# Scratch stores of a fused attention and two-MLP kernel: issued by GpSimd's queue instead of SyncE's

## The chip, the core and the metric

The kernel runs on one core of a Trainium2 chip. The core has TensorE (PE in the profile), VectorE (DVE), ScalarE (ACT), GpSimd (POOL) and SyncE (SP), each with its own in-order queue of instructions, and 16 DMA engines that they share. The metric is the time of one execution in device microseconds. Three runs of the kernel before gave 866.27, 866.44 and 866.68 us; the median is 866.44.

## The reference

Three stages, all in float32. `q`, `k`, `v` are drawn for 4 batches, 8 heads, 576 positions and a head size of 64.

```
scores = (q @ k^T) / 8, only where 0 <= row - column < 64, else -1e9
attn   = softmax(scores) @ v               -> x: 2304 tokens x 512
h = x @ w_in   (512 x 2048);  r = max(h, 0);  x = (r * r) @ w_out   (2048 x 512)
h = x @ w2_in  (512 x 2048);  g = max(h, 0) + log1p(exp(-|h|));  out = g @ w2_out
```

## The kernel before

**Precision.** Every matmul operand of the two MLPs is held as two float32r parts, a high part and the rest ("split"), and each product takes three matmuls: high x high, high x low, low x high. For a weight this split is made on ScalarE and VectorE in `add_weights`: `magnitude` (ACT, L498), `hold` and `shift` (DVE, L501 and L505, one input each), `top` and `bottom` (DVE, L511 and L517, two inputs), `hi` (ACT, L524) and `lo` (DVE, L528). There are 32 weight pieces per MLP: 16 of `w_in` (index 0 in the names) and 16 of `w_out` (index 1).

**Stages.** The attention works on 18 pairs of 64-row windows. The first MLP takes the tokens in five tiles of 384, 384, 512, 512 and 512. For the first two tiles the split weights of the first MLP stay in SBUF and are used there directly (matmuls L841, L842, L844 into `h`, then L863 into `acc`). While this goes on, each split weight is also stored to scratch memory in HBM: `w_in` to `d_in` (tiles `di...`) and `w_out` to `d_out` (tiles `do...`). Then sums and differences of quarters of `w_in` are made (`add_sums`, L570 to L601) and stored there as well: from the third tile on, the first product is done by a scheme with seven instead of eight products of half-size blocks, which needs these sums. From then on the weights come back from `di` and `do` through two rings of SBUF buffers (`ri`, loaded at L1277, and `ro`, loaded at L1285). The results of the first MLP go to scratch `yd` (L970) and are loaded for the second MLP at L987. The weights of the second MLP are split the same way, but later, in the middle of the first MLP's work, through three slots of an SBUF `area`: a slot is loaded (L474 or L479), split in place, stored, and free for the next weight only when that store has landed.

**What sets the order.** A planner (`Plan`) orders all work before the program is emitted, from written-down costs, due times (`WANTED`) and shifts (`SHIFT`). Every engine then runs its instructions in that order, and an instruction that waits holds up all behind it on its engine. In the kernel before, all DMAs are issued by SyncE (`nc.sync.dma_start`): loads and stores stand in one queue. A DMA also waits until the eighth DMA before it on its queue kind has landed, since eight semaphores serve each kind in turn.

**The stores.** There are 176 store instructions to scratch: `put_mats` (L467, two a call) for the pieces of `w_in` with an even number and for the sums; L536 for those with an odd number; L533 for `w_out`; and L970 for the first MLP's results (8 for the two tiles of 384, 24 for the three of 512, which are cut at the edges of the second MLP's tiles). GpSimd only builds an identity matrix and masks at the start.

Of the kernel before, what the change touches and what calls it, by code (L numbers as in the profile page):

```python
# [148 lines left out]
class Plan:  # L149
# [16 lines left out]
    def add(self, key, on, fn, after=(), rank=None, take=(), give=(), lag=0.17, close=(), choice=None, opens=(), then=None):  # L166
        j = Job()
        j.key, j.fn, j.rank, j.lag = key, fn, rank, lag
        j.on = dict(on)
        j.choice = choice  # L170
        j.close = list(close)
        j.opens = list(opens)
        j.after = [a for a in after if a is not None]
        j.take, j.give = list(take), list(give)
        j.then, j.nexts = then, []
        j.got, j.users, j.start, j.end, j.ready, j.who = {}, [], None, None, 0.0, None
        assert key not in self.jobs, key
        self.jobs[key] = j
        return key
# [117 lines left out]
def window_attention_moe_moe2(  # L297
# [22 lines left out]
    nc = tc.nc  # L320
# [10 lines left out]
    Q = 2 * P  # L331
# [18 lines left out]
    def f32(ap):  # L350
        return ap.bitcast(F32)
# [54 lines left out]
    live = {}  # L406
    whole = {"area": area}

    def place(j, name, shape, dtype):

        s = j.got[name]
        if isinstance(s, tuple):
            n = 1
            for d in shape[1:]:
                n *= d
            t = whole[s[0]][:, s[1]:s[1] + n]
            if dtype is not F32:
                t = t.bitcast(dtype)
            if len(shape) == 3:
                t = t.rearrange("p (a b) -> p a b", a=shape[1])  # L420
        else:
            of = ppool if s[0] == "p" else wpool if s[0] == "w" else pool
            t = of.tile(shape, dtype, tag=s, name=name.replace(".", "_"))
        live[name] = t
        return t
# [7 lines left out]
    def copy(e, out, in_):  # L433
        (nc.scalar.copy if e == "ACT" else nc.vector.tensor_copy)(out=out, in_=in_)  # L434
# [4 lines left out]
    def as_float(word):  # L439
# [11 lines left out]
    MAT = (  # L451
        {"A": 0, "T2": 1, "T3": 2, "T1": 3, "B": 4, "C": 5, "T4": 6},
        {"A": 0, "T1": 1, "B": 2, "T2": 3, "T3": 4, "T4": 5, "C": 6},
    )
    d_in = {
        (ph, b): dpool.tile([P, 7, 2, Q], F32, tag=f"di{ph}_{b}", name=f"di{ph}_{b}") for ph in range(2) for b in range(NB)
    }
    d_out = {
        (ph, b): dpool.tile([P, 2, 2, DM], F32, tag=f"do{ph}_{b}", name=f"do{ph}_{b}") for ph in range(2) for b in range(NB)
    }  # L460
# [3 lines left out]
    def put_mats(b, ph, first, step, t):  # L464

        for i in range(2):
            nc.sync.dma_start(  # L467
                out=d_in[ph, b][:, first:first + step + 1:step, i], in_=f32(t[:, i]).rearrange("p (m f) -> p m f", m=2)
            )

    def load_raw(t, ph, f, which):
        src = (W_IN, W_OUT)[which][ph].bitcast(U32)
        if which == 0:
            nc.sync.dma_start(  # L474
                out=t.rearrange("p (c f) w -> p c (f w)", c=KC),
                in_=src[:, f * 2 * P:(f + 1) * 2 * P].rearrange("(c p) f -> p c f", p=P),
            )
        else:
            nc.sync.dma_start(out=t.rearrange("p f w -> p (f w)"), in_=src[f * P:(f + 1) * P, :])  # L479

    def add_weights(ph, n, f, which, want):

        me = f"{ph}_{f}_{which}"
        z = f"z{me}"
        raw = f"raw{me}"

        def load(j):
            if ph:
                t = place(j, raw, [P, 2 * DM], F32)
                live["w" + me] = t.bitcast(F32R).rearrange("p (s f) -> p s f", s=2)  # L490
                t = t.bitcast(U32).rearrange("p (f w) -> p f w", w=2)
            else:
                t = wpool.tile([P, DM, 2], U32, tag=f"w{which}_{f}", name=raw)
            live[raw] = t
            load_raw(t, ph, f, which)

        def magnitude(j):
            nc.scalar.activation(out=place(j, z, [P, DM], F32), in_=live[raw][:, :, 1].bitcast(F32), func=AF.Abs)  # L498

        def hold(j):  # L500
            nc.vector.tensor_scalar(out=live[z], in0=live[z], scalar1=HUGE, scalar2=TINY, op0=ALU.min, op1=ALU.max)  # L501

        def shift(j):
            u = live[z].bitcast(U32)
            nc.vector.tensor_scalar(  # L505
                out=u, in0=u, scalar1=3, scalar2=0x3FFFFFFF, op0=ALU.logical_shift_left, op1=ALU.bitwise_and
            )

        def top(j):
            u = live[z].bitcast(U32)  # L510
            nc.vector.scalar_tensor_tensor(  # L511
                out=u, in0=live[raw][:, :, 1], scalar=0xC0000000, in1=u, op0=ALU.bitwise_and, op1=ALU.bitwise_or
            )

        def bottom(j):
            u = live[z].bitcast(U32)
            nc.vector.scalar_tensor_tensor(  # L517
                out=u, in0=live[raw][:, :, 0], scalar=29, in1=u, op0=ALU.logical_shift_right, op1=ALU.bitwise_or
            )

        def hi(j):
            if not ph:
                wt[f, which] = live["w" + me] = wpool.tile([P, 2, DM], F32R, tag=f"w{which}_{f}", name=f"w{me}")
            nc.scalar.copy(out=live["w" + me][:, 0], in_=live[z])  # L524

        def lo(j):
            t = live["w" + me]
            nc.vector.tensor_tensor(out=t[:, 1], in0=live[z], in1=f32(t[:, 0]), op=ALU.subtract)  # L528

        def store(j):  # L530
            t = live["w" + me]
            if which:
                nc.sync.dma_start(out=d_out[ph, f // 2][:, f % 2], in_=f32(t))  # L533
            elif f % 2:

                nc.sync.dma_start(out=d_in[ph, f // 2][:, MAT[ph]["T4"]], in_=f32(t[:, :, Q:]))  # L536
            else:
                put_mats(f // 2, ph, 0, MAT[ph]["B"], t)


        late = which == 1 and f >= LATE
        add(
            f"LW{me}", {"DMA": 1.52}, load, ["SS0_7" if ph else f"K0_0_{f - AHEAD}" if late else None],
            take=[("c", None, 1, [raw])] if ph else [], lag=3.2 if ph else 2.2,
            close=[("pro", (f"w1_{f}", 512 * i)) for i in range(2)] if not ph and late else [],
        )
        add(f"A{me}", {"ACT": 0.55}, magnitude, [f"LW{me}"], take=[("s", f"z{ph}", 1, [z])])
        add(f"B{me}", {"DVE": 0.34}, hold, [f"A{me}"])
        add(f"C{me}", {"DVE": 0.34}, shift, [f"B{me}"], lag=0.0)
        add(f"D{me}", {"DVE": 0.6}, top, [f"C{me}"], lag=0.0)  # L550
        add(f"E{me}", {"DVE": 0.6}, bottom, [f"D{me}"])
        add(f"F{me}", {"ACT": 0.54}, hi, [f"E{me}"])
        last = add(
            f"G{me}", {"DVE": 0.6}, lo, [f"F{me}"], give=[] if ph and not which else [z], rank=want if ph else None,
        )

        add(
            f"SW{me}", {"DMA": 1.52 if which or f % 2 == 0 else 0.78}, store, [last], give=[raw] if ph else [], rank=want, lag=4.0,
        )
        return last  # L560
# [56 lines left out]
    def tile_of(p):  # L617
        t = max(i for i in range(len(TILES[0])) if T0S[0][i] <= p * P)
        return t, p - T0S[0][t] // P
# [207 lines left out]
    yd = {u: dpool.tile([P, KC, u[1] - u[0]], F32, tag=f"y{u[0]}", name=f"yd{u[0]}") for u in units_y}  # L827

    def units_in(t0, t1):
        return [u for u in units_y if t0 <= u[0] and u[1] <= t1]  # L830
# [126 lines left out]
    def add_result1(t, after, at):  # L957

        T = TILES[0][t]

        def take_out(c):
            def fn(j):
                copy(j.who, place(j, f"r{t}_{c}", [P, T], F32), live[f"acc0_{t}_{c}"][:, 0:T])
            return fn

        def store(c):
            def fn(j):
                t0 = T0S[0][t]
                for u in units_in(t0, t0 + T):
                    nc.sync.dma_start(out=yd[u][:, c], in_=live[f"r{t}_{c}"][:, u[0] - t0:u[1] - t0])  # L970
            return fn

        cost = {"ACT": 0.44, "DVE": 0.5} if T == 384 else {"ACT": 0.54, "DVE": 0.62}
        for c in range(KC):
            add(
                f"RH{t}_{c}", cost, take_out(c), [after], at, [("s", "y", 1, [f"r{t}_{c}"])], [f"acc0_{t}_{c}"],
            )
            add(f"Dr{t}_{c}", {"DMA": 0.9}, store(c), [f"RH{t}_{c}"], at, give=[f"r{t}_{c}"], lag=2.5)
# [358 lines left out]
    for p in range(NPAIR):  # L1337
        t, o = tile_of(p)
# [99 lines left out]
    for n, (ph, t, b, i, at, step) in enumerate(uses):  # L1438
# [22 lines left out]
        else:  # L1461
            sums = add_block2(t, b, at, mats, ins[n], give_ins[n], x_names)
            for o, (k, h) in enumerate(((0, 0), (1, 1), (1, 0), (0, 1))):
                f = 2 * b + k
# [57 lines left out]
```

## Time and profile before

| | before |
|---|---|
| median of 3 runs | 866.44 us |
| the profiled execution | 868.16 us, of which the span of its instructions is 866.4 us |
| PE busy | 850.8 us (98%) |
| DVE busy | 724.2 us (84%) |
| ACT busy | 616.3 us (71%) |
| POOL busy | 3.6 us, all at the start |
| DMA packets | 225.97 MB, mean 261 GB/s over the span |
| granted TensorE clock | 0.998 |

The profiled execution took 868.16 us, 1.72 us more than the median of the runs without a profile; 1.76 us of it lie outside the span. Times in rows count from the start of the span. Busy time is that of an engine's instructions; an engine that issues a DMA is not busy by it. Idle time is put down to what ended it.

### The profile page before, as it was taken

What the parts mean: (1) busy time and instruction counts of PE and PEld (TensorE: products, weight loads), DVE (VectorE), ACT (ScalarE), POOL (GpSimd) and SP (SyncE); (2) the same over time, 40 slices, a digit from 0 to 9 for tenths busy, and PEclk for the clock granted to TensorE, in tenths of its full rate; (3) what the DMA queues carried; (4) which work ended last, traced back from release to release, by engine and by line L of the source; (5) the groups of instructions that cost most, each with busy time, mean ns of one, the idle gap of its engine ahead of it and who ended that gap; (6) DMA issues with size and microseconds to landing.
All of it is one profiled execution on the core that took longest, in us unless ns stands there. A gap on an engine that the chain in (4) does not pass through costs nothing.

```text
span 866.4 us, 16055 instructions
## 1 busy us (share of the span) xinstructions
PE 850.8 (98%) x5688; PEld 770.1 (89%) x5688; DVE 724.2 (84%) x1389; ACT 616.3 (71%) x1413; POOL 3.6 (0%) x19
## 2 busy tenths in 40 slices
PE   8899999999999999999999999999999999999998
PEld 6699999999988998898999888888889898899896
DVE  6999998798799998899467999999876678776675
ACT  7997776674678676675445888888776678676675
POOL 1000000000000000000000000000000000000000
PEclk9999999999999999999999999999999999999999
DMA  9999866999999899997999999894756551664521
GB/s 214 299 304 368 308 236 213 301 314 312 383 246 334 244 367 289 316 341 260 337 346 353 329 315 335 325 340 153 231 177 205 170 193 40 204 208 161 191 101 73
DMA packets 158575, 225.97 MB, mean 261 GB/s; under 512 B 64544, under 2 KB 115744, under 8 KB 158496
## 3 DMA queue, kind: packets, MB, share of 16 engines
q1 hardware_dynamic: 158496, 224.96, 79.3%
q8 instruction: 45, 0.74, 0.3%
q14 instruction: 34, 0.28, 0.1%
HBM read 169.35 MB, written 55.57 MB: 260 GB/s over the span
## 4 chain that ended last, share of the span: by engine, by line
PE 80%; DVE 8%; DMA 6%; SPq 3%; issue 1%; ACT 1%; DVEq 0%; ACTq 0%
PE acc L863 20%; PE acc L886 20%; PE pa L1074 16%; PE pb L1074 7%; PE pd L1074 5%; PE h L841 2%; PE h L842 2%; PE h L844 2%; SPq L643 2%; PE po L745 2%; DMA raw<-in_moe_w_in_dram 2%; PE pp L726 1%; SPq L474 1%; PE sc L682 1%; DVE gl L914 1%
## 5 line engine op out<-in xcount | busy, mean ns | idle before, releaser
L886 PE MATMUL acc<-ro,gh 128*128 128x512 f32 x576 | 178.9, 391 | 0.0
L886 PEld LDWEIGHTS acc<-ro,gh 128*128 128x128 f32 x576 | 107.2, 188 | 18.6
L863 PE MATMUL acc<-gh,ro 128*128 128x512 f32 x384 | 120.4, 395 | 0.0
L886 PE MATMUL acc<-ro,gl 128*128 128x512 f32 x288 | 113.8, 395 | 0.0
L863 PEld LDWEIGHTS acc<-gh,ro 128*128 128x128 f32 x384 | 69.1, 188 | 13.0 <-issue 0.7
L863 PE MATMUL acc<-gl,ro 128*128 128x512 f32 x192 | 74.9, 390 | 0.0
L914 DVE TENSOR_TENSOR gl<-l,gh 128x384 fp32r<-128x384 f32 x96 | 53.1, 553 | 23.3 <-ACT gh L911 22.4
L911 ACT CAST gh<-l 128x384 fp32r<-128x384 f32 x96 | 48.7, 507 | 24.6 <-DVE l L1261 10.6
L863 PE MATMUL acc<-gh,w 128*128 128x384 f32 x256 | 66.0, 338 | 0.0
L886 PEld LDWEIGHTS acc<-ro,gl 128*128 128x128 f32 x288 | 54.0, 188 | 11.7 <-DVE gl L914 0.3
L1074 PE MATMUL pa<-hxT,ri 128*128 128x384 f32 x288 | 62.0, 336 | 0.0
L1074 PE MATMUL pb<-xT,ri 128*128 128x256 f32 x432 | 60.6, 285 | 0.2 <-DVE wk L1116 0.2
L1257 DVE SCALAR_TENSOR_TENSOR e<-u,e 128x384 f32<-128x384 f32 x96 | 52.8, 550 | 6.2 <-ACT u L1247 6.2
L1074 PEld LDWEIGHTS pb<-xT,ri 128*128 128x128 f32 x432 | 55.9, 191 | 2.0 <-DVE wk L1116 0.4
L1261 DVE TENSOR_TENSOR l<-l,e 128x384 f32<-128x384 f32 x96 | 52.9, 553 | 4.2 <-ACT e L1243 0.5
L1074 PEld LDWEIGHTS pa<-hxT,ri 128*128 128x128 f32 x288 | 51.7, 188 | 2.8
L1252 ACT ACTIVATE l<-u 128x384 f32<-128x384 f32 x96 | 50.3, 524 | 2.7 <-DVE u L1249 1.4
L1074 PE MATMUL pa<-xA,ri 128*128 128x256 f32 (+1 forms) x288 | 51.1, 313 | 0.8 <-ACT c L434 0.6
L1243 ACT ACTIVATE e<-e 128x384 f32<-128x384 f32 x96 | 50.3, 524 | 1.8
L1178 ACT COPY wk<-pa 128x384 f32<-128x384 f32 x72 | 34.2, 475 | 22.8 <-PE pa L1074 22.7
L1074 PEld LDWEIGHTS pa<-xA,ri 128*128 128x128 f32 x288 | 45.3, 189 | 4.1 <-ACT c L434 0.9
L1239 ACT ACTIVATE e<-c 128x384 f32<-128x384 f32 x61 | 31.9, 523 | 23.5 <-DVE c L1186 22.6
(240 smaller groups left out, 2014.1 us busy)
## 6 DMA issues: line engine op xcount, KB each, us to landing
ri<-di SPq DMA_DIRECT2D x126, 512.0 KB, 5.6
ro<-do SPq DMA_DIRECT2D x76, 512.0 KB, 5.4
ri<-di SPq DMA_DIRECT2D x42, 256.0 KB, 3.9
raw<-in_moe_w_in_dram SPq DMA_DIRECT2D x16, 512.0 KB, 9.0
raw<-in_moe_w_out_dram SPq DMA_DIRECT2D x16, 512.0 KB, 6.7
do<-w SPq DMA_DIRECT2D x16, 512.0 KB, 5.3
di<-osa SPq DMA_DIRECT2D x32, 256.0 KB, 6.1
di<-osb SPq DMA_DIRECT2D x32, 256.0 KB, 6.1
```

Of the source, the lines that this page charges most:

```text
L643: nc.sync.dma_start(out=t[done:done + n], in_=src[b, :, s:s + n, :].rearrange("h p d -> p h d"))
L863: nc.tensor.matmul(o, lh, rh, start=n == 0 and k == 0, stop=n == NF - 1 and k == 2)
L886: nc.tensor.matmul(o, lh, rh, start=begins and k == 0, stop=ends and k == 2)
L911: nc.scalar.copy(out=place(j, f"gh{me}", [P, T], F32R), in_=live[src])
L914: nc.vector.tensor_tensor(out=place(j, f"gl{me}", [P, T], F32R), in0=live[src], in1=f32(live[f"gh{me}"]), op=ALU.subtract)
L1074: nc.tensor.matmul(out, w[:, s, c, :], x[k][:, c, :], start=(i == 0 and not on), stop=(i == 5), skip_group_check=on)
L1178: nc.scalar.copy(out=live[f"wk{me}"][:, i], in_=live[f"pa{me}"])
L1239: nc.scalar.activation(out=e, in_=live[src], func=AF.Abs)
L1243: nc.scalar.activation(out=e, in_=e, func=AF.Exp, scale=-1.0)
L1252: nc.scalar.activation(out=live[f"l{me}"], in_=live[f"u{me}"], func=AF.Ln)
L1257: nc.vector.scalar_tensor_tensor(out=e, in0=u, scalar=1.0, in1=e, op0=ALU.subtract, op1=ALU.subtract)
L1261: nc.vector.tensor_tensor(out=live[f"l{me}"], in0=live[f"l{me}"], in1=live[f"e{me}"], op=ALU.add)
```

## The change

All four stores to scratch memory move from SyncE's queue to GpSimd's. Loads stay on SyncE, and so do the stores of the final output (L1299). The planner's costs, due times and shifts are the same.

```diff
     def put_mats(b, ph, first, step, t):
         for i in range(2):
-            nc.sync.dma_start(
+            nc.gpsimd.dma_start(
                 out=d_in[ph, b][:, first:first + step + 1:step, i], in_=f32(t[:, i]).rearrange("p (m f) -> p m f", m=2)
             )
...
             if which:
-                nc.sync.dma_start(out=d_out[ph, f // 2][:, f % 2], in_=f32(t))
+                nc.gpsimd.dma_start(out=d_out[ph, f // 2][:, f % 2], in_=f32(t))
             elif f % 2:
-                nc.sync.dma_start(out=d_in[ph, f // 2][:, MAT[ph]["T4"]], in_=f32(t[:, :, Q:]))
+                nc.gpsimd.dma_start(out=d_in[ph, f // 2][:, MAT[ph]["T4"]], in_=f32(t[:, :, Q:]))
...
                 for u in units_in(t0, t0 + T):
-                    nc.sync.dma_start(out=yd[u][:, c], in_=live[f"r{t}_{c}"][:, u[0] - t0:u[1] - t0])
+                    nc.gpsimd.dma_start(out=yd[u][:, c], in_=live[f"r{t}_{c}"][:, u[0] - t0:u[1] - t0])
```

The instructions of PE, DVE and ACT stay the same, in the same order. SyncE's queue loses the stores. This is the place where the first MLP's weights are loaded and stored (`di`, `do` are scratch, `w_2_1` is `w_out` piece 2, `w_1_0` is `w_in` piece 1, `raw` is a weight as it was given):

```order
 L643 DMA q_990<-in_q_dram 128x8x64
@@ -47,60 +46,21 @@
 L479 DMA raw_5_1_1019<-in_moe_w_out_dram 128x1024
 L643 DMA v_1041<-in_v_dram 128x8x64
-L533 DMA do_1_94<-w_2_1_1012 128x1024
-L536 DMA di_0_77<-w_1_0_715 128x2x256
-L533 DMA do_0_93<-w_0_1_866 128x1024
 L479 DMA raw_6_1_1092<-in_moe_w_out_dram 128x1024
-L533 DMA do_1_94<-w_3_1_1069 128x1024
-L533 DMA do_0_93<-w_1_1_938 128x1024
 L479 DMA raw_7_1_1141<-in_moe_w_out_dram 128x1024
```

The load of `raw_6_1` stood behind three stores there, each of which waited for a split, and now stands behind a load. On GpSimd the same stores follow the masks:

```order
10 L387 AFFINE_SELECT masks<-masks 64x64 x12
11 L467 DMA di_0_77<-w_0_0_688 128x2x256 x2
12 L533 DMA do_1_94<-w_2_1_1012 128x1024
13 L536 DMA di_0_77<-w_1_0_715 128x2x256
14 L533 DMA do_0_93<-w_0_1_866 128x1024
15 L533 DMA do_1_94<-w_3_1_1069 128x1024
```

The first store, that of `w_in` piece 0, stood behind some forty loads on SyncE and now stands behind the masks alone; from there on the stores keep their order among themselves. The third place is on SyncE again, where the second MLP's weights go through the three slots of `area`, just ahead of its first tile:

```order
 L1285 DMA ro_1_5960<-do_0_101 128x1024
-L533 DMA do_1_102<-area 128x1024
-L467 DMA di_5_90<-osa_5_5977 128x2x256 x2
 L1277 DMA ri_3_6020<-di_0_85 128x512
 L1277 DMA ri_0_6024<-di_1_86 128x1024
@@ -335,8 +234,5 @@
 L474 DMA area<-in_moe_w_in_dram 128x4x256
 L1277 DMA ri_2_6089<-di_1_86 128x1024
-L533 DMA do_1_102<-area 128x1024
```

The store that empties a slot of `area` stood in the same queue as the ring loads and as the load that fills the slot again (L474); now only loads are left there, and that load waits for a store of the other queue.

## Rows read from the trace of the kernel before

**Rows 1.** The page's busy time of each engine, with share and instructions.
```profile
PE 850.8 (98%) x5688; PEld 770.1 (89%) x5688; DVE 724.2 (84%) x1389; ACT 616.3 (71%) x1413; POOL 3.6 (0%) x19
```

**Rows 2.** Windows: stretch, its length, then the columns that the first line names.
```profile
core 0: us, PE busy (x) PEld busy (x) DVE busy (x) ACT busy (x) POOL busy (x), PEclk, DMA share, GB/s
...
40.00:50.00 10.00, 9.36 (x105) 8.03 (x104) 9.93 (x22) 9.89 (x32) 0.00 (x0) 1.00 1.08 362
...
57.00:130.00 73.00, 73.00 (x503) 71.77 (x502) 72.97 (x148) 56.69 (x121) 0.00 (x0) 1.00 0.87 298
130.00:475.00 345.00, 343.67 (x2727) 313.78 (x2726) 288.36 (x535) 218.60 (x523) 0.00 (x0) 1.00 0.94 309
475.00:595.00 120.00, 118.51 (x589) 105.30 (x589) 116.17 (x232) 100.52 (x207) 0.00 (x0) 1.00 0.91 317
...
800.00:866.40 66.40, 62.65 (x308) 55.58 (x306) 41.59 (x82) 42.74 (x88) 0.00 (x0) 1.00 0.35 119
```

**Rows 3.** Waits of PE: who waited for whom, us, times, longest.
```profile
PE h L842 <- DVE w L528: 1.2, 2, 0.6
```

**Rows 4.** DVE, 84 to 110 us: start, duration, instruction, count.
```profile
88.79 1.88 DVE L528 TENSOR_TENSOR w<-z,w 128x512 fp32r<-128x512 f32 x3
90.60 0.75 DVE L501 TENSOR_SCALAR z<-z 128x512 f32<-128x512 f32 x2
91.27 0.74 DVE L505 TENSOR_SCALAR z<-z 128x512 uint32<-128x512 uint32 x2
...
97.17 0.41 DVE L501 TENSOR_SCALAR z<-z 128x512 f32<-128x512 f32 x1
...
106.81 0.67 DVE L528 TENSOR_TENSOR w<-z,w 128x512 fp32r<-128x512 f32 x1
```

**Rows 5.** PE, 104 to 109 us, the same columns.
```profile
107.81 0.60 PE L863 MATMUL acc<-gh,w 128*128 128x384 f32 x2
```

**Rows 6.** DVE groups by line and shape: count, busy us, mean ns, idle before.
```profile
L505 DVE TENSOR_SCALAR z<-z 128x512 uint32<-128x512 uint32 x53 | 21.7, 415 | 0.2
L501 DVE TENSOR_SCALAR z<-z 128x512 f32<-128x512 f32 x53 | 21.6, 414 | 4.7 <-ACT z L498 4.7
L528 DVE TENSOR_TENSOR w<-z,w 128x512 fp32r<-128x512 f32 x32 | 21.2, 675 | 0.0
```

**Rows 7.** Windows of L501 alone: stretch, length, DVE busy (count), clock, DMA share, GB/s.
```profile
57.00:130.00 73.00, 9.36 (x24) 1.00 0.87 298
...
475.00:595.00 120.00, 5.43 (x13) 1.00 0.91 317
```

**Rows 8.** Windows of L1249 alone, the same columns.
```profile
475.00:595.00 120.00, 2.81 (x8) 1.00 0.91 317
```

**Rows 9.** SyncE, 430 to 610 us: first and last store after 475 us, of 30.
```profile
486.53 0.37 SPq L536 DMA_DIRECT2D di<-area  x1
...
592.96 0.32 SPq L533 DMA_DIRECT2D do<-area  x1
```

**Rows 10.** Line L533 on SyncE: count, duration in ns (least/median/most), first and last start.
```profile
L533 SPq DMA_DIRECT2D do<-w x16: 319/332/1293, 64.8 to 129.2; - x16
```

**Rows 11.** Line L467 on SyncE, the same columns.
```profile
L467 SPq DMA_DIRECT2D di<-w x16: 360/688/1374, 57.2 to 110.2; - x16
```

**Rows 12.** DVE, 33 to 52 us: start, duration, instruction.
```profile
41.26 0.68 DVE L528 TENSOR_TENSOR w<-z,w 128x512 fp32r<-128x512 f32 x1
```

**Rows 13.** Chain of waits, 26 to 62 us: start, duration, what.
```profile
40.25 8.18 DMA raw<-in_moe_w_in_dram
```

**Rows 14.** Waits of SyncE's queue: who for whom, us, times, longest.
```profile
SPq L1277 <- PE pa L1074: 154.0, 65, 22.7
...
SPq L533 <- DVE area L528: 23.2, 9, 4.4
SPq L533 <- DVE w L528: 19.9, 8, 4.3
...
SPq L474 <- DMA do<-area: 2.6, 1, 2.6
```

**Rows 15.** Chain of waits, 455 to 480 us.
```profile
458.78 8.65 DMA do<-area
467.46 0.03 issue
467.49 6.82 DMA area<-in_moe_w_in_dram
```

**Rows 16.** DMA issues: queue, count, KB each, median us to landing.
```profile
ri<-di SPq DMA_DIRECT2D x126, 512.0 KB, 5.6
...
do<-area SPq DMA_DIRECT2D x16, 512.0 KB, 4.8
```

**Rows 17.** Waits of ACT, the columns of rows 3.
```profile
ACT z L498 <- DMA area<-in_moe_w_in_dram: 7.5, 3, 3.5
```

## The prediction

> **What bounds the kernel now.** I read the page's busy times first: PE works 98% of the span, GpSimd 3.6 us of it [rows 1]. Then the windows, to see where the missing 2% lie. From 57 to 130 us PE is busy 73.00 of 73 us; from 130 to 475 it lacks 345 - 343.67 = 1.33 us, from 475 to 595 it lacks 1.49 us, and the 3.75 us that it lacks after 800 us belong to the end, where no moved store is left [rows 2]. The first store is issued at 57.2 us [rows 11], so what lies before is touched only by stores that may now leave earlier. A smoother flow of transfers can thus give back 1.33 + 1.49 = 2.8 us at most, 0.33%.
>
> What the kernel can lose is not capped like that. The second column to read in the same rows is DVE: 72.97 of 73 us in the first stretch, 116.17 of 120 in the third. In both PE and DVE are full together. In the first, DVE splits weights that PE needs at once: shortly before it PE still waited openly for the split L528 [rows 3], and in it, around 107 us, one such split ends at 106.81 + 0.67 = 107.48 us [rows 4] while the group of matmuls that reads this weight starts at 107.81 [rows 5]: 0.3 us of lead. What DVE loses there beyond that lead, PE loses, and a PE that is full afterwards never gets it back.
>
> **What the change removes, adds and moves.** No work of PE, DVE or ACT changes. 176 stores leave SyncE's queue; their bytes are the same and go through the same 16 DMA engines, which are at 0.87 to 0.94 of their time in these stretches [rows 2].
>
> *DVE beside GpSimd.* In the first stretch 40 stores are issued (16 of `w_out`, 24 of `w_in`: two for each of 8 even pieces, one for each of 8 odd ones), and 30 from 475 us on [rows 9]. GpSimd must now write each of them out while DVE works, and no row shows the two together, since GpSimd is idle after the first microseconds [rows 2]. The instructions of DVE that could lose by it are the one-input ones: L501 and L505 take 414 and 415 ns for 128x512 where the two-input L528 takes 675 [rows 6], so they use SBUF at a higher rate than the rest. My assumption is that such an instruction is held up when it comes while GpSimd writes out a store. The price of one hold lies between 0 and 0.69 us, the median time that SyncE spends on a store of L467 [rows 11], waits and queueing included; the nearest row for the bare work is the least time of L533, 0.32 us [rows 10]. I take 0.33.
>
> How often: there are 24 pairs of L501 and L505 in the first stretch [rows 7]. A store is released by L528, so a pair is hit when it comes just behind one. From 84 to 110 us, read row by row, 8 of L501 start: 3 of them as a split ends, 2 more within 0.6 us. So three L528 end at 88.79 + 1.88 = 90.67 us and two L501 and two L505 follow at 90.60 and 91.27, while the L501 at 97.17 follows no split closely [rows 4]. I take half. That is 12 x 0.33 = 4.0 us, less the lead of 0.3: +3.7 us. With every pair hit at 0.69 it is 16.6 us, with no hold 0.
>
> From 475 to 595 us there are 13 + 13 such instructions and 8 of L1249 [rows 7, 8], together 34. GpSimd writes 30 x 0.33 = 10 us of 120, so 8% of them, 3, are hit, by half a hold on average where nothing ties them to a store: +0.5 us (0 to 34 x 0.33 = 11).
>
> From 130 to 475 us DVE has 345 - 288.36 = 57 us to spare [rows 2]; I count holds there at nothing, and if that cover fails the 19 pairs cost 19 x 0.33 = 6 us at most.
>
> The Trainium skill has a rule on this, in "SBUF — State Buffer", section "Who interferes with whom": VectorE in a two-port mode and GpSimd share a pair of SBUF ports, and whichever comes first keeps the other out for a whole instruction; single-input float32 copies and scalar operations can run in that mode. Rows 6 agree that these instructions run faster than two-input ones; that GpSimd holds them up no run here shows. With the 620 ns that the page's section "A bandwidth-pool intuition that's wrong" gives for a GpSimd-issued DMA alone, 24 pairs would cost, as an estimate, 24 x 0.62 = 15 us.
>
> *Stores that leave earlier.* The first weight's split ends at 41.26 + 0.68 = 41.9 us [rows 12], but its two stores went at 57.2 because SyncE was still busy with loads. On GpSimd they go at 42 us: 2 x 256 KB into DMA engines that move 362 GB/s at a share of 1.08 [rows 2], while the chain of waits runs through a weight load issued at 40.25 [rows 13]. That is 0.52 MB / 362 GB/s = 1.4 us if all of it delays that load, 0 if none. I take the middle, +0.7.
>
> *Loads that no longer stand behind stores.* SyncE waited 23.2 + 19.9 us for splits at L533 alone [rows 14]. Most of what stood behind were ring loads, and these have a deep cover: SyncE waits 154 us for PE to free their buffers [rows 14], while a load lands in 5.6 us [rows 16] and PE never waits for one. The loads that count are those into `area`: one waited for a store that took 8.65 us to land behind ring loads [rows 15], and ACT waited up to 3.5 us for such a load [rows 17]. In a queue of its own that store may land in nearer to the usual 4.8 us [rows 16]. Of the 1.49 us that PE lacks there I take a third: -0.5.
>
> *Stores that land later.* What a store written out by GpSimd takes to land no row shows. Where a slot of `area` waits for it (2.6 us in one place [rows 14]) a later landing costs what the earlier issue gives. Zero, with 2 us to either side.
>
> **Sum.** 3.7 + 0.5 + 0.7 - 0.5 = +4.4 us. On the profiled execution: 868.16 + 4.4 = 872.6. The runs without a profile stand 1.72 us below it, so the forecast for their median is 866.44 + 4.4 = 870.8 us.
>
> **Rivals.** *No hold.* DVE's instructions keep their times, and what is left is 0.7 - 0.5: 866.6 us, no change. For it: nothing in the trace shows a hold, and PE never waits for a ring load, so rearranged transfers stay hidden. Against it: no slack of DVE anywhere in the first stretch, so even 2 us of holds would show.
>
> *Faster.* Loads of `area` and of `q`, `k`, `v` leave SyncE up to 4 us earlier, the slots empty earlier, and the idle time of PE from 130 to 595 us goes: 2.8 us at most, 2 of them likely, giving 864.4. It decides if ACT's and DVE's in-order waits on late loads were the cause of those gaps. For it: the 8.65 us landing on the chain [rows 15]. Against it: the DMA engines are at 0.91 to 0.94 whoever issues [rows 2]. The Trainium skill says in "DMA: Bandwidth & Descriptors", section "Issuing engines are not separate DMA queues", that several issuing engines share the 16 DMA engines and save only issue time. The DMA share in rows 2 agrees that there is little to win from a second queue.
>
> *Late landings.* Stores written out by GpSimd land some 2 us later, the three slots of `area` turn round more slowly, the splits of the second MLP come late into a DVE that is already full, and two or three late weights cost PE 1 us each: 869. It needs a landing beyond 7 us, the usual 4.8 and 2 more.
>
> **How the numbers follow.** The forecast has 0.55, no hold 0.27, faster 0.13, late landings 0.05. A measurement of this kernel can tell about 0.2% (1.7 us) from no change. In the forecast's case the time lies between 868.2 and 883 (16.6 us in the first stretch, all pairs hit); it holds nearly all of slower: 0.52, with 0.05 from late landings and 0.02 from no hold: 0.59. The same: 0.25 from no hold, 0.03 from small holds: 0.28. Faster: 0.13. The range runs from 864.8 to 883: below it most of the outcomes of *faster* are left out, above it holds longer than 0.69 us.
>
> **What would show it.** Right: L501 and L505 between 57 and 130 us take longer than 415 ns or start after a gap with nothing to wait for, most of them just behind an L528; PE shows waits for L528 (`w`) or for `gl` in that stretch, which had none; and the stretch, not the later ones, holds most of the loss. The stores of L467 for the first weight go near 42 us. Wrong: L501 and L505 stay at 414 and 415 ns and PE stays full from 57 to 130 us; then the time is within 2 us of before, and its sign comes from the gaps between 340 and 595 us. If instead GpSimd's own queue backs up, so that stores leave later than they did on SyncE, the loss would lie at the rings' first loads and at the slots of `area`, and my placing of it would be wrong.

## The result, and where the time went

The changed kernel takes 875.67 us (median of 4 runs, 874.80 to 876.37); the kernel before, run beside it, 866.56. The ratio is 1.0098, 95% interval 1.0083 to 1.0113: 9.1 us slower, where I had forecast 4.4. The time lies in the range; the mechanism that I priced is not the one that cost it.

The page's busy times of the kernel after, beside [rows 1]:

```profile
PE 853.1 (98%) x5688; PEld 771.0 (88%) x5688; DVE 725.2 (83%) x1389; ACT 616.7 (71%) x1413; POOL 124.6 (14%) x195
```

GpSimd now spends 121 us writing out stores, and DVE's total grows by 1.0 us only. The windows of after, the columns of [rows 2]:

```profile
57.00:130.00 73.00, 72.43 (x500) 71.41 (x497) 72.59 (x146) 56.22 (x120) 28.94 (x38) 1.00 0.84 291
130.00:475.00 345.00, 339.74 (x2690) 309.17 (x2689) 282.50 (x528) 216.54 (x519) 69.14 (x102) 1.00 0.91 305
475.00:595.00 120.00, 118.56 (x600) 105.83 (x599) 116.19 (x229) 97.71 (x201) 20.82 (x33) 1.00 0.90 321
```

The loss is in the middle stretch, which I had costed at nothing: PE lacks 5.26 us of 345 there, against 1.33 before. The 0.57 us that it lacks from 57 to 130 us are one wait at 58 us, for a load of `q` and not for a split: PE came there 0.8 us earlier than in the trace before, and the load landed at 58.34 instead of 58.26 us. To find the places I laid PE's matmuls of both traces side by side, each with its place in the program, and subtracted the starts. The difference jumps at few places: +1.4 us at 224 us of the trace before, +3.0 from 351 to 354, +1.7 from 457 to 463, +0.7 at 608; the small rest is -0.4. Together 6.4 us, of 873.0 - 866.4 = 6.6 us between the two spans. (The two profiled runs lie 1.6 us above and 0.9 us below the medians of their kernels; that is the rest of the 9.1.) PE's waits of after; of these, the view of [rows 3] has only the third before, with 0.3 us:

```profile
PE tq L654 <- DMA q<-in_q_dram: 2.1, 2, 1.5
...
PE pa L1074 <- ACT wk L434: 1.2, 1, 1.2
PE tk L654 <- DMA k<-in_k_dram: 1.1, 1, 1.1
...
PE acc L863 <- ACT gh L911: 0.7, 1, 0.7
```

They go back to three transfers that land late, but for the 0.6 us at 58 us, which are among the first row's 2.1. (The 0.7 us at 608 I have not followed.) First, the chain of waits of after around 224 us (start, duration, what):

```profile
215.47 8.31 DMA di<-osa
...
223.88 0.07 ACT osa L597
...
224.40 0.59 ACT wk L434
...
225.03 1.69 PE pa L1074 x12
```

The store of a sum (`osa`, block 5 of the first MLP) leaves GpSimd at 215.47 us; on SyncE it left at 215.53. There it stood ahead of two loads of `ro` and landed at 221.33; now those two loads are issued before it on the other queue and run beside it, and it lands at 223.78. ScalarE, in order, stands at L597 for its buffer, and the copy `wk` that PE needs stands behind that.

Second, the chain around 351 us, PE's windows there (PE busy, granted clock, DMA share, GB/s), and the windows of the kernel before with the columns of [rows 2]:

```profile
344.30 10.11 DMA k<-in_k_dram
...
354.55 0.73 PE tk L654 x4
```

```profile
351.00:352.00 1.00, 0.29 (x3) 1.00 1.14 382
352.00:353.00 1.00, 0.21 (x2) 1.00 1.12 387
353.00:354.00 1.00, 0.42 (x4) 1.00 1.02 379
354.00:355.00 1.00, 0.46 (x5) 0.97 1.04 371
355.00:356.00 1.00, 1.00 (x5) 0.50 1.17 311
```

```profile
349.00:351.00 2.00, 1.12 (x11) 0.94 (x10) 1.33 (x4) 1.97 (x12) 0.00 (x0) 1.00 0.55 172
351.00:353.00 2.00, 1.75 (x11) 1.42 (x12) 1.78 (x4) 1.14 (x6) 0.00 (x0) 1.00 0.91 258
```

The load of `k` for the last pair takes 10.1 us from issue to landing (8.6 before). PE works 1.38 of the 4 us from 351 on, first waiting for `q` and then for `k`, and then the granted clock is 0.50, the lower of the two levels, from 354.9 to 358.3 us. The kernel before waits at the same place, 0.88 + 0.25 = 1.13 us, at a clock of 1.00. A wait of 1.5 us more than before thus costs 3.0, since the matmuls behind it run at half speed (seven of L863 start 0.2 us later each).

Third, at 457 us of the trace before, a load of the chain, and then ScalarE and PE in after:

```profile
451.76 9.53 DMA area<-in_moe_w_in_dram
```

```profile
461.31 0.66 ACT L498 ACTIVATE z<-area 128x512 f32<-128x512 f32 x1 [1.16 <-DMA area<-in_moe_w_in_dram]
461.88 0.60 ACT L911 CAST gh<-halvesw 128x512 fp32r<-128x512 f32 x1
```

```profile
462.53 0.73 PE L863 MATMUL acc<-gh,ro 128*128 128x512 f32 x2 [0.72 <-ACT gh L911]
```

A load into `area` takes 9.5 us (before, the same load 7.8) beside a 512 KB store that GpSimd issued at 449.46. ScalarE stands at L498 for it, and the `gh` that PE waits for comes right behind.

### The profile page after: what moved, and what is told of

Its sections match the earlier page's. It is cut to its first block, busy times and chain, and to the rows that moved or that the text cites. A ratio compares the mean times of both kernels' runs of the same rounds, so it can differ in the third digit from the quotient of the medians.

```text
span 873.0 us, 16173 instructions
## 1 busy us (share of the span) xinstructions
PE 853.1 (98%) x5688; PEld 771.0 (88%) x5688; DVE 725.2 (83%) x1389; ACT 616.7 (71%) x1413; POOL 124.6 (14%) x195
## 4 chain that ended last, share of the span: by engine, by line
PE 76%; DMA 6%; DVE 6%; SPq 4%; issue 3%; ACT 2%; POOL 1%; DVEq 0%; ACTq 0%; POOLq 0%
PE acc L863 19%; PE acc L886 18%; PE pa L1074 16%; PE pb L1074 7%; PE pd L1074 5%; SPq L474 2%; PE h L841 2%; PE h L844 2%; PE h L842 2%; SPq L643 2%; DMA k<-in_k_dram 1%; PE po L745 1%; PE sc L682 1%; PE pp L726 1%; DMA st<-yd 1%
## 5 line engine op out<-in xcount | busy, mean ns | idle before, releaser
L863 PE MATMUL acc<-gh,ro 128*128 128x512 f32 x384 | 121.8, 398 | 0.7 <-ACT gh L911 0.7
L863 PEld LDWEIGHTS acc<-gh,ro 128*128 128x128 f32 x384 | 69.9, 191 | 14.1 <-ACT gh L911 0.9
L863 PE MATMUL acc<-gl,ro 128*128 128x512 f32 x192 | 75.5, 393 | 0.3 <-DVE gl L914 0.3
L863 PE MATMUL acc<-gh,w 128*128 128x384 f32 x256 | 66.0, 338 | 0.0
```

The lines of the kernel that those rows point to most:

```text
L863: nc.tensor.matmul(o, lh, rh, start=n == 0 and k == 0, stop=n == NF - 1 and k == 2)
```

## Two theories

*Transfers*: on SyncE's queue the stores stood in one line with the loads, and a store that was not urgent came after the loads ahead of it. In a queue of their own they take a share of the DMA engines without waiting for those loads, and the load that PE or ScalarE needs next lands 1 to 3 us later. The rivals: *hold*, the main step of the prediction, and *slow stores*, that each store written out by GpSimd costs its part wherever it is. Twelve kernels were run, in three groups of four, each group beside runs of the kernel before (865.4 to 871.6 us, medians 867.2 to 867.4). Microseconds beside a ratio are its part of 867 us; by this measure the whole change, 1.0098, costs 8.5 us. The intervals are of 95%. Those with a switch in the code are one or a few lines longer, so their line numbers stand 1 to 5 higher. In the first 50 us profiled runs differ by up to 2 us even where the program is the same; steps of PE are therefore counted from 60 us on.

## Experiments: one kind of store at a time

The kernel before, with the queue chosen per kind of store (one line of each edit):

```diff
 e1  +            e = nc.sync if ph else nc.gpsimd      # first MLP's weights
 e2  +  put_mats(b, ph, first, step, live[f"o{n}{me}"], nc.gpsimd)   # sums
 e3  +            e = nc.gpsimd if ph else nc.sync      # second MLP's weights
 e4  +  nc.gpsimd.dma_start(out=yd[u][:, c], ...)       # first MLP's results
```

> Only the 40 stores of the first MLP's weights (L467, L533, L536 of the first phase) go to GpSimd's queue. Theory *transfers*: the loss of the whole change comes from three places at which a load or a store lands late (224, 351 and 457 us), and none of these stores is near them, so this part costs 0 to 0.5 us: 866 to 867 us, PE full from 57 to 130 us. Theory *hold* (the prediction's): nearly all of the loss is here, 3.7 us in the stretch from 57 to 130: about 870 us. Theory *slow stores* (each store written out by GpSimd costs its share, 9.1 us / 176): 40 of 176, 2.1 us, 868.6 us.

Measured: 1.0016 (1.0007 to 1.0024), +1.4 us. PE has no step from 60 to 337 us; it loses 0.9 us at 337 and has them back at 351. The window of 57 to 130 us of e1, and there L501 and L505 alone (DVE busy, count, clock, DMA share, GB/s), the latter's row of before last:

```profile
57.00:130.00 73.00, 73.00 (x487) 71.94 (x489) 73.00 (x147) 56.10 (x117) 28.54 (x37) 1.00 0.85 292
57.00:130.00 73.00, 9.75 (x24) 1.00 0.85 292
57.00:130.00 73.00, 9.88 (x24) 1.00 0.85 292
```

```profile
57.00:130.00 73.00, 9.58 (x24) 1.00 0.87 298
```

With the 9.36 us of [rows 7], L501 lengthens by 0.39 us and L505 by 0.30: 0.69 us over 48 instructions, where the prediction had 4.0, and PE stays full. Not even all of that need be holds: the two-input L528 takes longer too, 679 ns in the median instead of 673. *Hold* is out as the main cause. The 1.4 us are clear of noise all the same; the trace does not show where they go.

> Only the 64 stores of the sums (L467 from add_sums, both phases) go to GpSimd's queue. *Transfers*: the late landing at 224 us (ACT stands at L597 for a store of osa) comes with these stores, 1.4 us, and the two osa stores at 347 and 349 us take a part of the 3 us at 351: 868 to 870 us. *Hold*: no pair of L501 and L505 from 57 to 130 us is near one of them, at most 0.5 us: 867 us. *Slow stores*: 64/176 of 9.1 us = 3.3 us, 869.8 us, but without a step at 224 us.

Measured: 1.0021 (1.0010 to 1.0032), +1.8 us, with a step of 1.3 us at 224 us and one of 0.7 at 351: *transfers* by place; the amount is at the low end of its range.

> Only the 40 stores of the second MLP's weights (out of area) go to GpSimd's queue. *Transfers*: the store of 512 KB that then goes at 343.7 us, beside the loads of q and k for which PE waits, and the later slots of area make the steps at 351 and 457 us: 2 to 5 us, 869 to 871 us. *Hold*: 0.5 us, 867 us. *Slow stores*: 2.1 us, 868.6 us, spread.

Measured: 1.0079 (1.0060 to 1.0098), +6.8 us. Its window that holds both places, the columns as before; the kernel before had 128.67 us of PE in it:

```profile
345.00:475.00 130.00, 125.56 (x877) 112.43 (x874) 94.06 (x167) 73.61 (x149) 8.18 (x13) 0.99 0.93 323
```

Steps of 3.2 us at 351 to 354 and 1.9 at 457 to 463, as in the full change. *Transfers* again by place, and more than it expected: these 40 stores carry most of the loss.

> Only the 32 stores of the first MLP's results (L970) go to GpSimd's queue. *Transfers* and *hold*: nothing, 866.5 us within 0.7. *Slow stores*: 32/176 of 9.1 us = 1.7 us, 868.2 us.

Measured: 1.0038 (1.0026 to 1.0050), +3.3 us. All three expectations missed. The trace shows single steps of 0.2 to 0.6 us from 457 to 542 us, and that stores ran far ahead (those of the third tile at 302.6 us instead of 372.6). Which load each one hits I have not followed.

The four parts sum to 1.4 + 1.8 + 6.8 + 3.3 = 13.3 us, more than the whole.

## Experiments: the stores at the three places

Of each edit, what picks the queue:

```diff
 f1, f4: the whole change, but
 f1  +  e = nc.sync if (ph, f, which) == (1, 4, 1) else nc.gpsimd
     +  nc.sync if (ph, b, n) == (1, 3, "sa") else nc.gpsimd
 f4  +  these, (1, 2, 1), and all sums of (ph, b) == (0, 5)
 f2  the kernel before, with the three stores of f1 alone on nc.gpsimd
 f3  the same three on nc.scalar
```

> The whole change, but three of the 176 stores stay on SyncE's queue: do1_2 of the first of its two weights (512 KB, issued by GpSimd at 343.7 us) and the two of osa1_3 (256 KB each, 346.9 and 348.7). *Transfers*: the loads of q and k of the last pair no longer share the DMA engines with this 1 MB, PE's step at 351 to 354 us (3.0 us, of which 1.5 is waiting and 1.5 the halved clock behind it) goes: 875.7 - 3.0 = 872.7 us. *Slow stores*: 3/176 of 9.1 us = 0.2 us, 875.5 us, and the step stays.

Measured: 1.0037 (1.0024 to 1.0049) instead of 1.0098. The window of f1:

```profile
351.00:356.00 5.00, 5.00 (x34) 4.51 (x33) 3.74 (x8) 4.41 (x14) 0.19 (x1) 1.00 1.03 331
```

PE is full and the clock stays at 1.00; the steps at 224 and 457 us are still there. Three stores of 176 give back 0.61%, 5.3 us, against 0.2 by *slow stores*. That is more than the step of 3.0: in f1 PE does not have the wait of 1.1 us either that the kernel before has at this place.

> Only those three stores go to GpSimd's queue, the other 173 stay on SyncE's. *Transfers*: the step at 351 to 354 us comes with them, 2 to 3 us: 869 us. *Slow stores*: 0.2 us, no step: 866.8 us.

Measured: 1.0040 (1.0025 to 1.0055), +3.5 us, and PE's only large step after 60 us is 3.4 us at 351 to 354. As *transfers* had it, somewhat more.

> The same three stores go to ScalarE's queue, so a ring of its own but none that GpSimd writes out; the other 173 stay on SyncE's. *Transfers* (a second ring that takes a share of the DMA engines at once, whoever issues): the same step as with GpSimd, 2 to 3 us, 869 us, plus or minus 0.5 us for what ScalarE waits for the splits. *GpSimd's own way of issuing is to blame*: no step at 351, 866.8 us.

Measured: 1.0011 (0.9997 to 1.0025), no loss of PE at 351. That looks like the rival that blames GpSimd's own way of issuing, but it was not the same test: ScalarE, in order, issued the first store at 345.80 us, 2.3 us later than GpSimd in f2. So the question was put again, with GpSimd made as late:

```diff
 g1  +  nc.gpsimd.tensor_copy(out=ident16[:, 0:1], in_=f32(t)[:, 1, 0:1])
     +  for _ in range(10): nc.gpsimd.memset(ident16, 0.0)     # g2: 20
```

> As f2, the three stores alone on GpSimd's queue, but behind the split that the first of them waits for GpSimd first makes one small copy and 10 memsets of a constant that nothing reads any more, estimated at 2 us, so that it goes near 345.8 us, where ScalarE had issued it in f3. *Transfers* (it is when the packets come that counts, not who issues): the packets of q and k are mostly through by then as in f3, PE's step at 351 to 354 us falls from 3.4 us to 1 or less, 868 us. *GpSimd's own way of issuing*: the step stays at 3 us, 870.5 us.

> The same with 20 memsets, an estimated 4 us. *Transfers*: the step is gone, 867.4 us. *GpSimd's own way of issuing*: 870.5 us.

GpSimd in g1, and the windows of g1 at the place:

```profile
342.80 2.72 POOL L536 MEMSET ident<- 128x128 bf16 x10
345.57 0.70 POOL L538 DMA_DIRECT2D do<-area  x1
```

```profile
344.00:351.00 7.00, 7.00 (x72) 6.13 (x71) 5.79 (x11) 4.64 (x20) 3.35 (x9) 1.00 1.11 368
351.00:356.00 5.00, 5.00 (x54) 4.36 (x56) 3.07 (x7) 3.95 (x9) 0.00 (x0) 1.00 1.03 340
```

PE is full at 351 in g1, and has no loss there in g2 either (its trace loses 1.8 us at 365 instead, waiting for DVE and ScalarE; I have not followed what held these up). g2 takes 1.0011 (0.9999 to 1.0022): no loss that can be told from none. g1 takes 1.0026 (1.0007 to 1.0046), with twelve runs that fall into six from 866.07 to 869.08 and six from 870.54 to 873.54 us; the profiled one is of the lower six, and what the upper six do is not shown. The same queue and the same stores, 2 to 5 us later, and the step is gone from both traces: GpSimd's issuing alone does not make it, it is when the packets come. That another engine, issuing as early as GpSimd did, would cost as much was not run. SyncE's queue at this place in the kernel before (start, duration, instruction): the store stands behind both loads and is taken on only at 345.32 + 4.57 = 349.89 us.

```profile
342.38 0.53 SPq L643 DMA_DIRECT2D q<-in_q_dram  x1
343.09 2.14 SPq L643 DMA_DIRECT2D k<-in_k_dram  x1
345.32 4.57 SPq L533 DMA_DIRECT2D do<-area  x1
```

Issue and landing, in us, of each trace:

```
                  before         after          f2             f3             g1
load q         342.38 350.83  343.62 352.65  343.39 352.35  342.38 349.83  342.50 349.69
load k         343.09 351.71  344.30 354.41  344.10 354.53  343.09 350.67  343.20 350.36
store do1_2    345.32 353.00  343.73 351.99  343.54 351.52  345.80 351.96  345.57 351.82
```

And the packets that start in each microsecond, counted from the trace's packet records. Those of 256 bytes are the loads of `q` and `k`, those of 4096 in the other queue the store:

```
before  346..350   SyncE's queue, 256 B:  44 710 911 285  70
after   348..353   SyncE's queue, 256 B: 326 479 499 403 303  25
                   GpSimd's queue, 4 KB:  13  50  57  68  49  19
g1      346..350   SyncE's queue, 256 B:  84 843 892 229   0
                   GpSimd's queue, 4 KB:   0   0  11  77  97
```

Before, and in g1, 700 to 900 packets of `q` and `k` pass in a full microsecond; in after 300 to 500, as long as GpSimd's packets run beside them. The Trainium skill has the rule in "DMA: Bandwidth & Descriptors", section "Queues, rings and completion order": each DMA engine takes turns between the queues that have work for it, packet by packet. The counts agree that both queues move in the same microsecond; that the turns go packet by packet they do not show: from 349 to 350 us they are 479 beside 50. The prediction had weighed another section of that page, by which a second issuing engine saves only issue time, and had taken from it that there is little to win; what there is to lose it had not asked.

> Only the first store of do1_2 goes to GpSimd's queue; the two of osa1_3 and all others stay on SyncE's. *Transfers*: half the bytes beside the loads of q and k, so they land 1 to 2 us late instead of 3, and PE's step is 1 to 2 us: 868.5 us. If only GpSimd's stores of sums mattered: no step, 867.4 us.

Measured: 1.0021 (1.0009 to 1.0033), +1.8 us; `k` lands at 352.99, between before and f2. PE's step at 351 is 0.4 us in the trace, less than expected. Inconclusive in size, in direction as *transfers* had it.

> The whole change, but the eight stores at the three places stay on SyncE's queue: the three of before, the four of the sums of block 5 (first MLP; issued by GpSimd at 214.0 to 220.2 us) and the first store of do1_1 (449.5 us). *Transfers*: the steps at 224 us (1.4), at 351 to 354 (3.0) and at 457 (1.5) go: 875.7 - 5.9 = 869.8 us, 5% of the stores for two thirds of the loss. *Slow stores*: 8/176 of 9.1 us = 0.4 us, 875.3 us.

Measured: 1.0017 (1.0004 to 1.0030). Eight stores of 176 on SyncE's queue give back 7.0 of 8.5 us, and no step is left in the trace at 224, at 351 or at 457 us. The middle stretch of f4, where after had 339.74:

```profile
130.00:475.00 345.00, 344.93 (x2736) 315.34 (x2736) 289.63 (x537) 220.23 (x526) 66.64 (x99) 1.00 0.92 312
```

GpSimd still issues 168 stores in the whole kernel, some of every kind. With that *slow stores* is out.

> The whole change, but the 32 stores of the first MLP's results stay on SyncE's queue. Alone they cost 3.3 us (e4), spread over places after 450 us at which the stores run ahead. *The parts add up*: 875.7 - 3.3 = 872.4 us. *They overlap with the others* (the same loads are late already): 874.5 to 875.7 us.

The edit is `nc.sync` again at L970. Measured: 1.0099 (1.0084 to 1.0114), nothing gained, though these stores cost 3.3 us alone. The parts do not add up; how they overlap I have not followed.

No version beat the kernel before by its interval.

## The prediction, step by step

- **PE is the bound, and a smoother flow can give back 2.8 us at most.** Nothing speaks against it. f4's trace gets some of it (344.93 of 345 us), but not its median.
- **DVE beside GpSimd, +3.7 and +0.5 us.** This is the step that failed. L501 and L505 lengthen in the first stretch of e1 by 0.69 us instead of 4.0, and PE did not feel it; in after it waited for no split there. From 475 to 595 us PE lacks 1.44 us, 1.49 before. Over the whole of after they take 418 and 426 ns, against [rows 6]:

```profile
L505 DVE TENSOR_SCALAR z<-z 128x512 uint32<-128x512 uint32 x53 | 22.3, 426 | 0.2
L501 DVE TENSOR_SCALAR z<-z 128x512 f32<-128x512 f32 x53 | 21.7, 418 | 6.2 <-ACT z L498 6.2
```

  I had bounded the price from the time that SyncE spends on a store, and assumed that DVE is the one to wait. No row bore that out, and 0.55 of the chances rested on it. GpSimd spends 121 us on 176 stores, 0.69 us on each and not the 0.33 that I took: with twice the price the loss that it stood for still did not come. That the forecast has the right direction, and the range the time, is luck.
- **130 to 475 us: nothing.** Wrong, and for the reason given there: DVE's slack covers holds, it does not cover a load that lands late. All three large steps are in this stretch.
- **Stores that leave earlier, +0.7.** The step is of the right kind at the wrong place. The first weight's stores left at 40.35 us, as forecast for 42, and cost under 0.2 us of PE there (from 40 to 50 us it worked 9.18 us, 9.36 before). The stores that cost most are three that go from 343.73 on, beside the loads of the last pair, instead of behind them; I never asked of the other stores which load each would now run beside.
- **Loads that no longer stand behind stores, -0.5.** Not seen: the third of 1.49 us that the loads into `area` should have given back is 0.05. The loads of `q` and `k` left SyncE no sooner: they stand behind a ring load that waits for PE, before and after.
- **Stores that land later, 0 with 2 to either side.** Mis-sized: at 224 us a store lands 2.4 us later and PE loses 1.4. The median of `do<-area` went from 4.8 [rows 16] to 6.2 us:

```profile
do<-area POOLq DMA_DIRECT2D x16, 512.0 KB, 6.2
```

- **The rival "late landings", 869 us, chance 0.05.** The nearest to what happened, and too narrow: it thought of the stores alone, and wanted landings beyond 7 us. It is the loads beside them that cost more, and the halved clock behind PE's wait doubles the largest of them.
- **"Its sign comes from the gaps between 340 and 595 us."** Right for the two larger of the three steps, 224 us lies outside; the bound beside it, that the time would then be within 2 us of before, was wrong.

## What to carry to other kernels

When stores leave a queue that they share with loads, look for the loads that have little lead: list for each store that will go sooner, which load is in flight at that time and who waits for it. A shared queue is also an order of priority, and a second queue gives it up: here 8 of 176 stores cost 7.0 of 8.5 us. Where the granted clock falls behind a wait of TensorE, as it did at 351 us, the wait is to be priced with the matmuls behind it at the lower clock.

## What the runs showed of the hardware

GpSimd and DVE seem to get in each other's way, but by these rows GpSimd is the one that waits. GpSimd in after, and below it DVE in the same stretch:

```profile
82.16 2.11 POOL L533 DMA_DIRECT2D do<-w  x1 [4.17 <-DVE w L528]
...
90.32 1.65 POOL L533 DMA_DIRECT2D do<-w  x1
```

```profile
82.39 0.75 DVE L501 TENSOR_SCALAR z<-z 128x512 f32<-128x512 f32 x2
83.06 0.42 DVE L505 TENSOR_SCALAR z<-z 128x512 uint32<-128x512 uint32 x1
83.40 0.41 DVE L501 TENSOR_SCALAR z<-z 128x512 f32<-128x512 f32 x1
83.73 0.42 DVE L505 TENSOR_SCALAR z<-z 128x512 uint32<-128x512 uint32 x1
```

A store that takes 0.53 us at least takes 2.11 while five one-input instructions of DVE run back to back; over the sixteen of this form the mean is 803 ns, where the same stores out of `area` take 562:

```profile
L533 POOL DMA_DIRECT2D do<-w x16 | 12.8, 803 | 53.5 <-DVE w L528 45.6 <-DVE sm L717 4.1 <-DVE z L511 3.8
...
L533 POOL DMA_DIRECT2D do<-area x16 | 9.0, 562 | 117.2 <-DVE area L528 89.9 <-ACT wk L1178 12.0 <-DVE halvesw L501 6.8
```

That is 16 x 0.24 = 3.9 us, by chance what I had charged to DVE; GpSimd had the time. "SBUF — State Buffer", section "Who interferes with whom", in the Trainium skill lets whichever comes first keep the other out for a whole instruction; here the store began first, at 82.16 us, and still was the one to stretch, while the longest one-input instruction of DVE in this stretch took 0.56 us, 0.15 more than the others. No kernel was run that takes L501 and L505 away, so that they are the cause rests on these rows alone.

The other thing not expected is the size of the clock's part at 351 us: 1.5 of 3.0 us. Not every wait brings it: behind the 1.2 us at 224 us in after, and behind the 1.1 us at 350 us in the kernel before, the granted clock stayed at 1.00.
